# Recurrent attention and a gated feed-forward in one kernel: state matmuls ordered behind scores, one step begun by halves, the last rows stored in two parts, and a planner that counts changes of tile shape

## The chip, the cores and the metric

The kernel runs on one core of one Trainium2 chip. The metric is device time in microseconds (us), here the median of three runs. The core has five engines with instruction queues of their own that work side by side: TensorE (PE in the profile), VectorE (DVE), ScalarE (ACT), GpSimd (POOL) and SyncE (SP). PE multiplies matrices and writes to eight banks of PSUM; DVE, ACT and POOL work element by element; SP (and, for the weights, POOL) issues the DMA transfers. Each queue runs in its order; an instruction that waits for a semaphore holds up all that is behind it on its queue.

## The reference

First a linear recurrence per batch, head and feature, over 768 tokens, then a gated feed-forward over all tokens. There are 4 batches, 8 heads of width 48, and d_ff is 1536. Cut to what is computed:

```python
f = 1.0 / (1.0 + np.exp(-f_logit))
for t in range(S):
    state = f[:, :, t, :, None] * state + np.einsum('bhd,bhe->bhde', k[:, :, t], v[:, :, t])
    y[:, :, t] = np.einsum('bhd,bhde->bhe', q[:, :, t], state)
x = y.transpose(0, 2, 1, 3).reshape(B * S, H * D)          # 3072 x 384
out = (np.maximum(x @ w_gate, 0.0) * (x @ w_val)) @ w_out  # 3072 x 384
```

## The kernel before

The recurrence is done in chunks of 128 tokens. Within a chunk, cumulative sums of the log decay (the "cum" matmuls, L612, L613, L784) go through exponentials on ACT (`expo`, L625, L628, L794, L796), which scale keys and queries to `hats` (POOL L630, L806, L809; DVE L633). Keys and queries are transposed to `qkT`, in the first pass by PE (L664), later by DMA on SP (`turn`, L563). Scores are keys against queries (`scores`, L703 and L851), masked by DVE into `ptm` (L708, L858). Outputs come from masked scores and values (L736, L890) and from queries and the old state (`inter`, L719, and L886). The state is renewed by keys against values (`state`, L685 and L913), an addition on DVE (`ssum`, L581) and a multiply on POOL (`st`, L583).

The work is staged in six steps, `c` from 0 to 5 (the loop at L988). Each step makes 512 rows of `x`, transposed in `xT`, and runs the feed-forward over them: `ffn_hidden` for 12 blocks of d_ff (two groups of three matmuls at L937, relu on ACT at L943, product on DVE at L947 into `gT`), then `ffn_out` (12 matmuls at L966 for each of four blocks of 128 rows, a copy on ACT at L976, a store on SP at L980 from one of four buffers `osb`). Steps 0 to 3 get their rows from `attention_unit(d, b)`, which covers two chunks, 256 tokens, of one batch: pass `d` = 0 is steps 0 and 1, pass `d` = 1 is steps 2 and 3, with two units to a step. Steps 4 and 5 use `attention` for one chunk of all four batches. In steps 0 and 1 the feed-forward begins by halves (`groups`, L985): the first six blocks are done for the first unit's 256 columns, then for the second's, and the other six for all 512. The output part of a step is spread between the hidden blocks of the next one (`pend`); that of step 5 comes last.

No order is written out by hand. Every operation is added to a `Plan` with its engine, what it reads and writes, an occupancy and a latency in us, and a priority. `listed` (L181) then picks, again and again, the operation that can start earliest (ties by priority), on a model of five queues, the PSUM banks (with limits for each kind of use, L396) and the DMA rings; `needs` turns the result into semaphore waits. `chain` (L537) keeps operations of one line ("scores", "state", "intra", "ffn", ...) in order among themselves: each follows the one added before it. So the occupancies given at L691, L706, L748, L752, L755 and L851 decide how PE's work is interleaved, and, through it, the order on all other queues, the loads and stores of SP among them. Where the model has an early gap on PE, `fillers` puts matmuls on zeros (L1030).

Most matmuls use the array as one tile of 128 rows and 128 columns. The scores of a unit use 64x64 tiles, its state 64x128, `inter` 128x32, the outputs 64x32, and the scores of steps 4 and 5 64x128. In the model of this kernel a change from one tile shape to another costs nothing by itself; each operation's occupancy holds its own share.

`new_state(kv[0], ...)` is called right after the state matmuls are added; the state's second half, `new_state(kv[1], ...)`, at the end of the unit.

Of the kernel before, what the change touches and what calls it, by code (L numbers as in the profile page):

```python
# [11 lines left out]
class Op:  # L12
# [4 lines left out]
                 "after", "follows", "flow", "goal", "floor", "ring", "descs", "deps0", "ways")  # L17

    def __init__(self, eng, emit, reads, writes, occ, lat, prio, opens=(), after=(), follows=()):
        self.eng, self.emit, self.reads, self.writes = eng, emit, reads, writes  # L20
        self.occ, self.lat, self.prio, self.opens = occ, lat, prio, list(opens)
        self.after, self.follows = list(after), list(follows)
        self.users = []
        self.inc = False
        self.sem = None
        self.val = 0
        self.start = None
        self.flow = None
        self.ring = "hw"
        self.descs = 0  # L30
        self.floor = 0.0
        self.ways = {eng: (emit, occ, 0.0)}

# [81 lines left out]
class Plan:  # L115
# [9 lines left out]
    def add(self, eng, emit, reads=(), writes=(), occ=0.5, lat=0.2, prio=0, opens=(), after=(), follows=()):  # L125
        op = Op(eng, emit, list(reads), list(writes), occ, lat, prio, opens, after, follows)
        op.idx = len(self.ops)
        self.ops.append(op)
        return op
# [51 lines left out]
    def listed(self, banks, rings):  # L181
# [20 lines left out]
        left = len(self.ops)  # L202

# [8 lines left out]
        while left:  # L212
# [19 lines left out]
            op.eng, op.emit, op.occ = e, op.ways[e][0], op.ways[e][1]  # L232
            for tile, s in zip(op.opens, slot):
                if s["tile"] is not None:
                    for o in s["tile"].ops:
                        op.deps[o] = "war"
                s["tile"] = tile
                tile.ap, tile.slot = s["ap"], s
                used[tile.group] = used.get(tile.group, 0) + 1
# [80 lines left out]
def bass_hgrn2_outer__then__ffn_reglu_kernel(  # L320
# [216 lines left out]
    def chain(line, *args, **kw):  # L537

        last = tails.get(line)
        tails[line] = add(*args, follows=[last] if last else [], **kw)  # L540
        return tails[line]
# [44 lines left out]
    def attention_unit(d, b):  # L586
# [93 lines left out]
        def state():  # L680
            for p in range(NP):
# [8 lines left out]
        chain("state", "PE", state, hk_(h0) + hk_(h0 + 1) + [f"hats{h0 + i}" for i in range(2)] + [f"v_{v0 + i}" for i in range(2)],  # L690
              kv, occ=0.54, lat=PE_L, prio=P + 4, opens=kv)  # L691
        dk = [f"decu_{b}{j}" for j in range(2)]
        new_state(kv[0], 2 * d, b, w0, P, decu[:, b, 0, :, :], dk)
        pk = []
        for i in range(2):
# [10 lines left out]
            chain("scores", "PE", scores, [k_ for k_ in both if k_[-2] == "0" or k_.startswith(f"qkT{q0 + i}_")], sj, occ=0.29 if i else 0.38, lat=PE_L, prio=P + 5, opens=sj)  # L706
            for j in range(2):
# [4 lines left out]
                pk.append(f"ptm{m0 + i}_{j}")  # L712
        ys = [Bank("y"), Bank("y")]
# [32 lines left out]
        if late:  # L746
            chain("intra", "PE", outputs, both + old + [f"S{b}_0"] + pk + [f"{x}{v0 + i}" for x in ("v_", "vpad") for i in range(2)], ys,
                  occ=1.17 if d else 1.06, lat=PE_L, prio=P + 7, opens=ys)  # L748
        for half in range(0 if late else 2):
            chain("intra", "PE", lambda half=half: intra(half), pk[2 * half:2 * half + 2]  # L750
                  + [f"v_{v0 + half}", f"vpad{v0 + half}"] + (ys if half else []), ys,
                  occ=0.44 if half == 0 else 0.35, lat=PE_L, prio=P + 7, opens=ys if half == 0 else [])  # L752
        if not late:
            chain("inter", "PE", lambda: inter(1), both + [f"S{b}_0", ys[1]], [ys[1]],
                  occ=0.28, lat=PE_L, prio=P + 7)  # L755
# [76 lines left out]
    def attention(c, b):  # L832
# [9 lines left out]
        if b % 2 == 0:  # L842
# [11 lines left out]
            chain("scores", "PE", scores, qk_(qi) + qk_((w + 1) % NQ), both, occ=0.66, lat=PE_L, prio=P + 5, opens=both)  # L854
# [103 lines left out]
    def ffn_out(g, bs, cuts=1):  # L958
        gi = g % NG
        o = {b: Bank("f") for b in bs}  # L960
        for s in range(NJ // OJ):
            js = range(s * OJ, (s + 1) * OJ)
            for b in bs:
                def proj_out(b=b, js=js):
                    for j in js:
                        mm = te.matmul(o[b].ap[:, 0:DM], gT[gi][:, j, b * C:(b + 1) * C], wo[:, j, :],  # L966
                                       start=(j == 0), stop=(j == NJ - 1))
                    return mm
                P = (g + 1) * B * 10 + 5 + NJ * 3 + b * 3
                chain("ffn", "PE", proj_out,  # L970
                      [f"gT{gi}_{j}_{b}" for j in js] + sorted({w_key("wo", j) for j in js}), [o[b]],
                      occ=pe_t(*[DM] * OJ), lat=PE_L, prio=P + 1000, opens=[o[b]] if s == 0 else [])
        for b in bs:
            oi = (g * B + b) % NO
            P = (g + 1) * B * 10 + 5 + NJ * 3 + b * 3
            add("ACT", lambda b=b, oi=oi: sc.activation(osb[oi][:, :], o[b].ap[:, 0:DM], AF.Copy), [o[b]], [f"osb{oi}"],  # L976
                prio=P, **act_t(DM))
            row = ((2 * (g % 2) + b // 2) * S + (g // 2 * 2 + b % 2) * C) if g in units else b * S + g * C
            both = [(bass.AP(tensor=out.tensor, offset=row * DM, ap=[[DM, C], [1, DM]]), osb[oi][:, :])]
            op = add("SP", lambda both=both: [sy.dma_start(d, s_) for d, s_ in both], [f"osb{oi}"], [f"out{g}_{b}"],  # L980
                     occ=0.5, lat=0.9, prio=P)
            dma(op, f"osb{oi}", 0.7, len(both), 130)
# [3 lines left out]
              1: [(0, 2, range(0, 6)), (2, 4, range(0, 6)), (0, 4, range(6, NJ))]}  # L986
# [30 lines left out]
    for item in pend:  # L1017
        ffn_out(*item)
# [98 lines left out]
```

## Time and profile before

| | us |
|---|---|
| runs | 194.48, 194.25, 194.47 (median 194.47) |
| the profiled execution | 194.1 |
| its span | 192.4 |
| TensorE busy, share of the span | 183.7, 95% |
| VectorE, ScalarE, GpSimd busy | 109.5, 109.9, 67.6 |
| granted TensorE clock over the span | 1.0 |

The profile shows one execution. The span runs from the first to the last instruction; the execution's time has about 1.7 us around it. Busy times of engines lie beside one another and do not add up to the span. The ends of matmuls are modelled and overlap, so that a block's cost is the distance from its start to the next one's. A line such as "L937 PE MATMUL ps<-xT,wg 128*128 128x512 bf16 x3" names the line of the kernel, the engine, the output and inputs by the program's names, the tile (rows * columns), the moving operand's shape and the number of instructions. Most busy groups of the page, with mean durations:

| group | count | busy us | mean ns |
|---|---|---|---|
| L937 PE, hidden, gate and value, 512 columns | 360 | 97.4 | 379 |
| L937 PE, hidden, 256 columns | 144 | 23.6 | 273 |
| L966 PE, output, 384 columns | 288 | 52.1 | 326 |
| L736 PE, outputs of the units, tile 64x32 | 512 | 6.1 | 220 |
| L703 PE, scores, tile 64x64 | 256 | 5.1 | 219 |
| L685 PE, state, tile 64x128 | 128 | 4.2 | 204 |
| L719 PE, `inter`, tile 128x32 | 144 | 3.5 | 221 |
| L976 ACT, output copy, 384 columns | 24 | 11.8 | 490 |

### The profile page before, as it was taken

How to read it: one execution, taken by the hardware profiler on the slowest of the kernel's cores; microseconds unless marked ns; L12 is line 12 of the kernel's file. 1: busy time of each engine (PE TensorE's matmuls, PEld its weight loads, DVE VectorE, ACT ScalarE, POOL GpSimd, SP SyncE). 2: the span in 40 equal slices, each digit the busy share in tenths (PEclk: the TensorE clock that was granted, in tenths of full speed). 3: DMA queues.
4: the chain of work that ended last, by engine and by line, in shares of the span. 5: the costliest groups of instructions: out<-in, count | busy, mean ns of one | idle time of the engine just before them, and what ended most of it. 6: DMA issues, size and time to landing. Idle time of an engine off the chain costs nothing.

```text
span 192.4 us, 5447 instructions
## 1 busy us (share of the span) xinstructions
PE 183.7 (95%) x2291; PEld 108.9 (57%) x2291; DVE 109.5 (57%) x203; ACT 109.9 (57%) x232; POOL 67.6 (35%) x108
## 2 busy tenths in 40 slices
PE   7779797999999999999999999999999999999994
PEld 7657493556688645555556545555555455554552
DVE  5377555765899998965556546337238233344200
ACT  3867783468698777367396395485434433334322
POOL 8759460316465545435538408108100000000000
PEclk9999999999999999999999999999999999999999
DMA  5999999999959999997999889998540311011122
GB/s 159 316 257 266 245 207 210 243 260 278 280 102 264 211 253 209 234 201 160 215 171 198 171 188 227 157 207 191 88 95 29 85 41 39 2 41 41 44 81 82
DMA packets 93864, 32.46 MB, mean 169 GB/s; under 512 B 86928, under 2 KB 93840, under 8 KB 93840
## 3 DMA queue, kind: packets, MB, share of 16 engines
q1 hardware_dynamic: 89856, 28.58, 66.3%
q0 software_dynamic: 3984, 3.54, 11.3%
q8 instruction: 18, 0.29, 0.6%
q14 instruction: 6, 0.05, 0.1%
HBM read 25.95 MB, written 4.72 MB: 159 GB/s over the span
## 4 chain that ended last, share of the span: by engine, by line
PE 82%; DMA 12%; SPq 2%; POOL 1%; issue 0%; ACT 0%
PE ps L937 45%; PE ps L966 25%; DMA wv<-in_moe_w_val_dram 5%; DMA k_in<-in_k_dram 4%; DMA wg<-in_moe_w_gate_dram 3%; SPq L486 2%; PE ps L736 2%; PE ps L703 2%; PE ps L685 1%; PE ps L719 1%; PE ps L851 1%; POOL hats L630 1%; PE ps L890 1%; PE ps L664 1%; PE ps L886 1%; PE ps L784 1%
## 5 line engine op out<-in xcount | busy, mean ns | idle before, releaser
L947 DVE TENSOR_TENSOR gT<-relu,ps 128x512 bf16<-128x512 bf16 (+1 forms) x84 | 50.3, 607 | 54.2 <-PE ps L937 46.1
L943 ACT ACTIVATE relu<-ps 128x512 bf16<-128x512 f32 (+1 forms) x84 | 44.7, 536 | 31.5 <-PE ps L937 30.6
L937 PE MATMUL ps<-xT,wg 128*128 128x512 bf16 (+1 forms) x252 | 60.5, 349 | 1.2 <-DMA wg<-in_moe_w_gate_dram 0.9
L937 PE MATMUL ps<-xT,wv 128*128 128x512 bf16 (+1 forms) x252 | 60.5, 349 | 1.0 <-DMA wv<-in_moe_w_val_dram 1.0
L966 PE MATMUL ps<-wo,gT 128*128 128x384 bf16 x288 | 52.1, 326 | 0.0
L966 PEld LDWEIGHTS ps<-wo,gT 128*128 128x128 bf16 x288 | 27.1, 98 | 19.0
L937 PEld LDWEIGHTS ps<-xT,wv 128*128 128x128 bf16 x252 | 23.4, 98 | 21.4 <-DMA wv<-in_moe_w_val_dram 1.5
L937 PEld LDWEIGHTS ps<-xT,wg 128*128 128x128 bf16 x252 | 23.6, 98 | 19.9 <-DMA wg<-in_moe_w_gate_dram 1.1
L976 ACT ACTIVATE osb<-ps 128x384 f32<-128x384 f32 x24 | 11.8, 490 | 31.5 <-PE ps L966 31.5
L708 DVE TENSOR_TENSOR ptm<-ps,seen 128x512 bf16<-128x512 f32 x32 | 20.0, 680 | 3.2 <-PE ps L703 3.2
L630 POOL TENSOR_TENSOR hats<-k_in,expo 128x384 bf16<-128x384 f32 x16 | 15.9, 998 | 10.5 <-ACT expo L625 8.2
L583 POOL TENSOR_TENSOR st<-ssum,decu 128x384 bf16<-128x384 f32 x12 | 9.9, 830 | 18.4 <-DVE ssum L581 12.2
L806 POOL TENSOR_TENSOR hats<-k_in,expo 128x384 bf16<-128x384 f32 x8 | 7.8, 996 | 21.1 <-DMA k_in<-in_k_dram 17.2
L858 DVE TENSOR_TENSOR ptm<-ps,tri 128x512 bf16<-128x512 f32 x16 | 10.1, 682 | 1.2 <-PE ps L851 1.2
L581 DVE TENSOR_TENSOR ssum<-ps,st 128x384 f32<-128x384 f32 x16 | 8.7, 552 | 2.6 <-PE ps L913 1.9
L760 ACT ACTIVATE xT<-ps 128x384 bf16<-128x384 f32 x11 | 6.5, 606 | 5.7 <-PE ps L736 5.6
L639 POOL CAST vpad<-v_in 128x384 bf16<-128x384 f32 x16 | 8.5, 557 | 0.1
L601 ACT ACTIVATE f_in<-f_in 128x768 f32<-128x768 f32 (+1 forms) x9 | 6.8, 768 | 2.8 <-DMA f_in<-in_f_logit_dram 2.7
L809 POOL TENSOR_TENSOR hats<-q_in,expo 128x384 bf16<-128x384 f32 x8 | 7.8, 994 | 0.0
L633 DVE TENSOR_TENSOR hats<-q_in,expo 128x384 bf16<-128x384 f32 x8 | 7.7, 960 | 0.1
L625 ACT ACTIVATE expo<-ps 128x384 f32<-128x384 f32 x12 | 5.5, 488 | 3.2 <-PE ps L613 3.2
L603 ACT ACTIVATE bneg<-f_in 128x768 bf16<-128x768 f32 (+1 forms) x9 | 6.8, 768 | 0.1
(86 smaller groups left out, 166.8 us busy)
## 6 DMA issues: line engine op xcount, KB each, us to landing
f_in<-in_f_logit_dram SPq DMA_DIRECT2D x12, 384.0 KB, 5.1
k_in<-in_k_dram SPq DMA_DIRECT2D x12, 384.0 KB, 5.5
q_in<-in_q_dram SPq DMA_DIRECT2D x12, 384.0 KB, 5.6
v_in<-in_v_dram SPq DMA_DIRECT2D x12, 384.0 KB, 5.0
out_dram<-osb SPq DMA_DIRECT2D x24, 192.0 KB, 2.0
wo<-in_moe_w_out_dram POOLq DMA_DIRECT2D x3, 384.0 KB, 8.8
wg<-in_moe_w_gate_dram POOLq DMA_DIRECT2D x2, 288.0 KB, 6.5
wv<-in_moe_w_val_dram POOLq DMA_DIRECT2D x2, 288.0 KB, 7.2
```

The costliest lines, as they stand in the source:

```text
L581: add("DVE", lambda: ve.tensor_tensor(tmp[:, :], kv.ap[:, 0:HD], s_old[:, :], ALU.add), [kv, f"S{b}_{(c + 1) % 2}"], [key], prio=P + 8, ** ...
L583: add("POOL", lambda: gp.tensor_tensor(t4(s_new), t4(tmp), rate, ALU.mult), [key] + dk, [f"S{b}_{c % 2}"], prio=P + 8, occ=0.79, lat=0.23)
L630: add("POOL", lambda i=i, hi=hi, ei=ei: gp.tensor_tensor(hats[:, hi, 1, :, 0:D], by_i["k"][:, i, :, :], expo[:, ei, 1, :].rearrange("p (h ...
L639: add("POOL", lambda i=i, vout=vout: gp.tensor_copy(vout, by_i["v"][:, i, :, :].rearrange("p (n j) d -> p n j d", j=2)), key["v"] + [f"vpa ...
L708: add("DVE", lambda i=i, j=j, s=sj[j]: ve.tensor_tensor(ptm_all[:, m0 + i, j, :, :], s.ap[:, :].rearrange("p (n t) -> p n t", n=NP), seen[ ...
L806: add("POOL", lambda: gp.tensor_tensor(hk, kin[:, b % 2, :, :], ex[:, 1, :].rearrange("p (h d) -> p h d", h=H), ALU.mult), in_keys("k", c, ...
L858: add("DVE", lambda j=j, s=s: ve.tensor_tensor(ptm[mi][:, j, :, :], s.ap[:, :].rearrange("p (n t) -> p n t", n=NP), mask, ALU.mult), [s, " ...
L937: mm = te.matmul(bank.ap[:, 0:n], wt[:, kt, j * 128:(j + 1) * 128], xT[xi][:, b0:b1, kt, :], start=(kt == 0), stop=(kt == NK - 1))
L943: add("ACT", lambda: sc.activation(relu[ri][:, 0:n], gate.ap[:, 0:n], AF.Relu), [gate], [f"relu{ri}"], prio=P, **act_t(n))
L947: add("DVE", lambda: ve.tensor_tensor(gT[gi][:, j, n0:n1], relu[ri][:, 0:n], val.ap[:, 0:n], ALU.mult), [val, f"relu{ri}"], [f"gT{gi}_{j}_ ...
L966: mm = te.matmul(o[b].ap[:, 0:DM], gT[gi][:, j, b * C:(b + 1) * C], wo[:, j, :], start=(j == 0), stop=(j == NJ - 1))
L976: add("ACT", lambda b=b, oi=oi: sc.activation(osb[oi][:, :], o[b].ap[:, 0:DM], AF.Copy), [o[b]], [f"osb{oi}"], prio=P, **act_t(DM))
```

## The change

Five things change, all of them on the host, in what is added to the plan and what the plan reckons.

- An operation carries a tile shape. When the plan places an operation on PE whose shape differs from the last one's, it adds 0.095 us to its occupancy if the last was 128x128 and 0.14 us otherwise. The occupancies of the narrow operations are lowered in return.
- In pass 1 (steps 2 and 3) the state matmuls of a unit are added after its scores and must follow the last scores in the order (`behind`).
- Step 2's feed-forward begins by halves: its first three blocks of d_ff are done for the first unit's 256 columns, then for the second's, and the other nine for all 512.
- The last block of output rows (step 5, fourth block) is computed, copied and stored in two column parts, 0 to 192 and 192 to 384, each with its own bank, copy and store.
- `ffn_out` loops over parts, and the keys of `osb` and of the stores name the part; for the other blocks there is one part, 0 to 384.

```diff
+    def add(self, eng, emit, reads=(), writes=(), occ=0.5, lat=0.2, prio=0, opens=(), after=(), follows=(), tile="128x128"):
         op = Op(eng, emit, list(reads), list(writes), occ, lat, prio, opens, after, follows)
+        op.tile = tile
...
             op.eng, op.emit, op.occ = e, op.ways[e][0], op.ways[e][1]
+            if e == "PE" and op.tile != shape:
+                op.occ += 0.095 if shape == "128x128" else 0.14
+                shape = op.tile
...
-    def chain(line, *args, **kw):
+    def chain(line, *args, behind=(), **kw):
         last = tails.get(line)
-        tails[line] = add(*args, follows=[last] if last else [], **kw)
+        tails[line] = add(*args, follows=([last] if last else []) + list(behind), **kw)
...
-        chain("state", "PE", state, hk_(h0) + hk_(h0 + 1) + [f"hats{h0 + i}" for i in range(2)] + [f"v_{v0 + i}" for i in range(2)],
-              kv, occ=0.54, lat=PE_L, prio=P + 4, opens=kv)
         dk = [f"decu_{b}{j}" for j in range(2)]
-        new_state(kv[0], 2 * d, b, w0, P, decu[:, b, 0, :, :], dk)
+
+        def states():
+            chain("state", "PE", state, hk_(h0) + hk_(h0 + 1) + [f"hats{h0 + i}" for i in range(2)] + [f"v_{v0 + i}" for i in range(2)],
+                  kv, occ=0.315, lat=PE_L, prio=P + 4, opens=kv, tile="64x128",
+                  behind=[tails["scores"]] if d else [])
+            new_state(kv[0], 2 * d, b, w0, P, decu[:, b, 0, :, :], dk)
+        if not d:
+            states()
...
-            chain("scores", "PE", scores, [...], sj, occ=0.29 if i else 0.38, lat=PE_L, prio=P + 5, opens=sj)
+            chain("scores", "PE", scores, [...], sj, occ=0.215, lat=PE_L, prio=P + 5, opens=sj, tile="64x64")
...
+        if d:
+            states()
...
-                  occ=1.17 if d else 1.06, lat=PE_L, prio=P + 7, opens=ys)
+                  occ=0.94 if d else 0.8, lat=PE_L, prio=P + 7, opens=ys, tile="64x32")
...
-                  occ=0.44 if half == 0 else 0.35, lat=PE_L, prio=P + 7, opens=ys if half == 0 else [])
+                  occ=0.26, lat=PE_L, prio=P + 7, opens=ys if half == 0 else [], tile="64x32")
...
-                  occ=0.28, lat=PE_L, prio=P + 7)
+                  occ=0.14, lat=PE_L, prio=P + 7, tile="128x32")
...
-            chain("scores", "PE", scores, qk_(qi) + qk_((w + 1) % NQ), both, occ=0.66, lat=PE_L, prio=P + 5, opens=both)
+            chain("scores", "PE", scores, qk_(qi) + qk_((w + 1) % NQ), both, occ=0.43, lat=PE_L, prio=P + 5, opens=both, tile="64x128")
...
-    def ffn_out(g, bs, cuts=1):
+    def ffn_out(g, bs, cuts=(0, DM)):
         gi = g % NG
-        o = {b: Bank("f") for b in bs}
-        for s in range(NJ // OJ):
+        parts = list(zip(cuts, cuts[1:]))
+        o = {(b, z): Bank("f") for b in bs for z in parts}
+        steps = [(s, b, z) for z in parts for s in range(NJ // OJ) for b in bs]
+        for s, b, z in steps:
...
-                        mm = te.matmul(o[b].ap[:, 0:DM], gT[gi][:, j, b * C:(b + 1) * C], wo[:, j, :],
-                                       start=(j == 0), stop=(j == NJ - 1))
+                    mm = te.matmul(o[b, z].ap[:, 0:z[1] - z[0]], gT[gi][:, j, b * C:(b + 1) * C], wo[:, j, z[0]:z[1]],
+                                   start=(j == 0), stop=(j == NJ - 1))
...
-              1: [(0, 2, range(0, 6)), (2, 4, range(0, 6)), (0, 4, range(6, NJ))]}
+              1: [(0, 2, range(0, 6)), (2, 4, range(0, 6)), (0, 4, range(6, NJ))],
+              2: [(0, 2, range(0, 3)), (2, 4, range(0, 3)), (0, 4, range(3, NJ))]}
...
-        ffn_out(*item)
+        ffn_out(*item, cuts=(0, DM) if item != pend[-1] else (0, 192, DM))
```

## The prediction

> **What bounds the kernel now.** I read the page's totals first, then the chain of waits in order of time, then TensorE's timeline, then the tail.
>
> ```profile
> PE 183.7 (95%) x2291; PEld 108.9 (57%) x2291; DVE 109.5 (57%) x203; ACT 109.9 (57%) x232; POOL 67.6 (35%) x108
> PE 82%; DMA 12%; SPq 2%; POOL 1%; issue 0%; ACT 0%
> ```
> TensorE (PE) is busy 95% of 192.4 us; no other engine passes 57%. The chain (start, length, what) says where that holds:
>
> ```profile
> 21.32 9.57 DMA wv<-in_moe_w_val_dram
> 30.89 0.05 issue
> 30.94 3.41 PE ps L937 x15
> ...
> 181.71 7.81 PE ps L966 x48
> 189.53 0.02 issue
> 189.55 0.49 ACT osb L976
> ```
> Between 30.94 and 189.53 every piece of the chain is PE's. So there are three stretches: a head that ends when the last third of `wv` lands (30.89), 158.6 us in which only PE's own work counts, and a tail of 2.8 us.
>
> TensorE's timeline (start, duration, work) gives the price of a change of tile shape:
>
> ```profile
> 29.14 0.81 PE L937 MATMUL ps<-xT,wg 128*128 128x512 bf16 x3
> 30.94 0.82 PE L937 MATMUL ps<-xT,wv 128*128 128x512 bf16 x3 [0.98 <-DMA wv<-in_moe_w_val_dram]
> 46.67 1.46 PE L966 MATMUL ps<-wo,gT 128*128 128x384 bf16 x8
> 48.06 0.52 PE L685 MATMUL ps<-vpad,hats 64*128 64x96 bf16 x16
> 48.51 0.64 PE L703 MATMUL ps<-qkT 48*64 48x128 bf16 x32
> 49.08 0.82 PE L966 MATMUL ps<-wo,gT 128*128 128x384 bf16 x4
> 49.74 0.33 PE L612 MATMUL ps<-bneg,upto 128*128 128x384 bf16 x1
> 79.77 0.81 PE L937 MATMUL ps<-xT,wg 128*128 128x512 bf16 x3
> 80.51 0.51 PE L685 MATMUL ps<-vpad,hats 64*128 64x96 bf16 x16
> 80.96 0.82 PE L937 MATMUL ps<-xT,wv 128*128 128x512 bf16 x3
> ```
> Starts are to be read, since ends overlap. Three full matmuls of 512 columns advance the start by 0.65, but 79.77 to 80.51 is 0.74: entering a narrow tile costs 0.09. The first block after leaving is 0.01 longer (49.08 to 49.74 is 0.66, four 384-column matmuls elsewhere 0.65). From 48.06 to 48.51 one narrow block follows another of a different shape in the same 0.45 that L685 takes before a full-width block (80.51 to 80.96). So a narrow block next to a narrow block saves 0.104.
>
> **The change, part by part.**
>
> *Narrow blocks together.* With the new plan's instruction order beside the old one, I count after 30.94 how often PE goes from full width to narrow: 20 times before, 17 after (in three of the four units of pass 1 the state matmuls stand directly behind the scores, in the fourth behind the outputs, where before one of four stood beside scores). 3 x 0.104 = -0.31 us. Bounds: 3 x 0.09 and, if the new neighbours cost as much as a separate entry, 0.
>
> [...]
>
> *Step 2 by halves.* Three of the twelve blocks of d_ff are done per unit, 256 columns at a time: six groups (gate and value) become twelve of half width. Three 256-column matmuls take 0.328 (27.51 to 27.84 on the same timeline), three of 512 take 0.648: 6 x (2 x 0.328 - 0.648) = +0.05 on PE. The finer start gains nothing by itself, since PE has no idle time there to fill. Beside PE: ACT +6 x 0.386 - 3 x 0.596 = +0.53 and DVE +6 x 0.416 - 3 x 0.684 = +0.44. DVE is 80 to 90% busy from 48 to 82 us, but the new order brings 24 output matmuls (L966, no DVE work) into 75.7 to 80.3, so the load spreads; taken as hidden.
>
> *Last rows in two parts.* 12 matmuls of 384 columns (0.1625 each, 7.81/48) become 24 of 192. The 192-column matmuls at L612 start 0.08 apart: 24 x 0.0825 - 1.95 = +0.03. Then only the second half is exposed. ACT: 490 ns for 384 columns, 176 for 8 (L652), so 192 cost about 333: -0.16. The store:
>
> ```profile
> 190.40:190.80 0.40, 0.00 (x0) 0.00 (x0) 0.00 (x0) 0.00 (x0) 0.00 (x0) 1.00 0.00 0
> 190.80:191.00 0.20, 0.00 (x0) 0.00 (x0) 0.00 (x0) 0.00 (x0) 0.00 (x0) 1.00 0.39 154
> 191.00:191.20 0.20, 0.00 (x0) 0.00 (x0) 0.00 (x0) 0.00 (x0) 0.00 (x0) 1.00 1.03 392
> 191.20:191.40 0.20, 0.00 (x0) 0.00 (x0) 0.00 (x0) 0.00 (x0) 0.00 (x0) 1.00 1.03 384
> 191.40:191.60 0.20, 0.00 (x0) 0.00 (x0) 0.00 (x0) 0.00 (x0) 0.00 (x0) 1.00 0.17 54
> 191.60:192.00 0.40, 0.00 (x0) 0.00 (x0) 0.00 (x0) 0.00 (x0) 0.00 (x0) 1.00 0.00 0
> ```
> (Window, length, engines, clock, DMA share, GB/s.) Of the 2.3 us from ACT's end (190.04) to 192.4 the DMA engines work only about 0.6; the rest is fixed. Half the bytes per row in equally many rows: between 0 saved (if a row costs the same) and 0.3. I take -0.25. The first half's store is issued about 1 us earlier; an issue takes 0.34 on SP, so the second is not delayed.
>
> [...] Here four stores at L980 stand at 73.31, 73.98, 76.36 and 76.83 on SP and landed a median of 2.0 after issue, the last two plainly overlapped; so I take one fixed cost.
>
> *Planner's costs.* These move instructions but no work. Head: in the new order both halves of a unit's outputs (L736) stand behind the group that waits for `wg` at 21.07, so 0.33 of PE work moves behind that wait; POOL places its state multiply (0.84) after the first `wo` issue, which delays the key product at 24.32 by 0.84 and the transposes at 25.65 by perhaps 0.5. The cover is the 0.98 that PE idles for `wv` at 30.94. That transfer is issued at 21.32 on POOL's landing of `wg`, ahead of all that moved. Without the cover it would be +0.3 to +0.5; I take 0.
>
> *Waits that the new order can open after 30.94.* The four transposes that stood at 45.13 now come 0.65 earlier, at 44.48, and need the key product that POOL ends at 44.40: 0 to 0.2. State behind scores makes the state late: scores, four masks on DVE, `ssum` (L581), POOL's L583, then L719. From the start of scores: 0.29 + 0.22 (first half and its latency) + 2.47 (four L708) + 0.55 + 0.83 = 4.36. PE's work between, summed from the rows in the new order, is 4.9 in unit 0 and 4.7 in unit 1; unit 2 has 5.4 against 4.7 (one more gT product), unit 3 stands about 0.25 clear. Nothing stalls, but margins are 0.25 to 0.7. Old small stall for comparison: L719 at 72.90 starts 0.05 later than its entry price explains. I take +0.10 in all, bounds 0 and 0.9 (all four late by half a us, less their margins, and the four transposes).
>
> **Sum.** -0.31 + 0.05 + 0.03 + 0.10 - 0.16 - 0.25 = -0.54. The profiled execution took 194.1 (span 192.4, 1.7 around it), so 193.56; it lies 0.37 under the median 194.47, so in runs of that kind 193.93. Bounds of this case: 193.6 (no new wait, 0.3 at the store) to 194.5.
>
> **Rivals.**
>
> *The state's margin is eaten.* If DVE's masks and POOL's product come 0.5 later than summed (L630 on POOL takes 998 ns against L583's 830, DVE is near full), units 1 and 3 stall 0.15 and 0.25 and the transposes 0.1: +0.4 over my 0.1, 194.3. Against: the old order had equally tight places and lost 0.05.
>
> *Slower: step 4's first scores (L851) wait for their transposed keys and queries.* SP's order changes: the loads of q and v for step 4, and the next f, now stand behind the fourth output block of step 1, which ends on PE at 86.6; ACT 0.49, store 0.36, q issued at 87.5, landed 5.6 later at 93.1. The step's cumulative sums move from 86.1 to 91.5, so POOL's products begin at about 92.4, and the last input to a transpose is ready at 97.6. Its DMA transpose stands behind a k load (about 98) and lands 3.0 / 3.6 / 6.4 us after issue (least, median, most in the trace); an issue itself took up to 3.6. Scores stand at 104.6 on my sum, against 100.5. With median values there are 3 us left; with an issue at 100.5 and the longest landing it is 106.9, 2.3 late: 196.2. It turns slower from a landing at about 105.5. For it: loads fill the queue; against: scores themselves moved 4.1 later.
>
> *The change does not do what it says:* real neighbours cost as much as apart (the 0 bound), and only the tail gains: 194.25.
>
> **How the numbers follow.** My case 0.55, margin eaten 0.20, scores wait 0.15, tail alone 0.10. What a measurement can tell is 0.2%, 0.39 us: faster is below 194.08, slower above 194.86. My case is almost all faster, with a little of the fourth: 0.57; same 0.27 (the second, most of the fourth, the rim of mine); slower 0.16 (the third and the end of the second). Predicted 193.93; its own range 193.6 to 194.5; the range for 8 in 10 reaches into the slower rival to 195.2 and, for a landing of `wv` or a store that is luckier, down to 193.4.
>
> **What would show it.** Right: the chain still all PE from about 30.9, PE's last matmul at 189.3 to 189.4, narrow entries 17, the last ACT piece 0.33, the end about 2.4 after it begins. Wrong: a wait named at L719 (state) or L851 (transposes) on PE, idle over 0.98 before `wv`, or a last store that ends no sooner.

## The result and the profile after

| | before | after |
|---|---|---|
| runs, median us | 194.48 (7 runs) | 193.82 (7 runs, 193.47 to 193.93) |
| ratio after / before | | 0.9964, 95% interval 0.9952 to 0.9976 |
| profiled execution, its span | 194.1, 192.4 | 193.93, 192.2 |
| head: first group of 512 columns on `wv` starts | 30.94 | 31.45 |
| TensorE from there to the last output copy | 158.61 | 158.31 |
| tail: from that copy's start to the end of the span | 2.82 | 2.43 |

The changed kernel is 0.36% faster. The three lines at the bottom split each profiled span at the two places that the prediction used. They add up to -0.18, not to the -0.66 of the medians: before's profiled execution was one of its faster ones, after's one of its slower ones.

Totals and chain shares on the page of after (all lines are of `kernel.py` after the change: the hidden matmuls L937 are L950 now, the output L966 is L981, scores L703 L714, state L685 L691, `inter` L719 L732, warming L1030 L1046):

```profile
PE 185.4 (96%) x2326; PEld 114.5 (60%) x2326; DVE 109.1 (57%) x205; ACT 110.7 (58%) x237; POOL 68.3 (36%) x108
PE 91%; DVE 3%; ACT 2%; DMA 2%; issue 1%
```

The 12% of DMA in the chain are down to 2%: the head no longer ends with the landing of `wv`. TensorE's timeline of after shows what it ends with (start, duration, work, and in brackets the idle time ahead and what ended it):

```profile
26.19 0.39 PE L670 MATMUL ps<-ident,hats 128*128 128x128 bf16 x4
26.41 0.27 PE L950 MATMUL ps<-xT,wg 128*128 128x256 bf16 x1
27.63 0.39 PE L950 MATMUL ps<-xT,wg 128*128 128x256 bf16 x2 [0.94 <-issue]
...
30.80 0.81 PE L950 MATMUL ps<-xT,wg 128*128 128x512 bf16 x3
31.45 0.81 PE L950 MATMUL ps<-xT,wv 128*128 128x512 bf16 x3
```

TensorE stops for 0.94 us between the first and the second matmul of one group. They read the same tiles, and the second has no semaphore to wait for; the profile names nothing ("issue"). The `wv` group follows at 31.45 with no wait in front of it. Before, it waited 0.98 and started at 30.94.

After the head, the same timeline in step 2, with a narrow pair:

```profile
81.53 1.46 PE L981 MATMUL ps<-wo,gT 128*128 128x384 bf16 x8
82.93 0.64 PE L714 MATMUL ps<-qkT 48*64 48x128 bf16 x32
83.50 0.51 PE L691 MATMUL ps<-vpad,hats 64*128 64x96 bf16 x16
83.95 0.82 PE L981 MATMUL ps<-wo,gT 128*128 128x384 bf16 x4
```

Eight output matmuls take 1.30 by themselves and 1.40 here: one entry. Scores then take 0.57, as they did ahead of a full-width block (before, 78.53 to 79.11 was 0.58), and the state 0.45, as before: the second entry is gone and nothing has come in its place.

The end of the chain (start, length, what), and the windows of the tail (window, length, engines, clock, DMA share, GB/s):

```profile
181.90 7.84 PE ps L981 x60
189.74 0.02 issue
189.76 0.33 ACT osb L991
```
```profile
190.10:190.50 0.40, 0.00 (x0) 0.00 (x0) 0.00 (x0) 0.00 (x0) 0.00 (x0) 1.00 0.48 158
190.50:190.90 0.40, 0.00 (x0) 0.00 (x0) 0.00 (x0) 0.00 (x0) 0.00 (x0) 1.00 0.00 0
190.90:191.10 0.20, 0.00 (x0) 0.00 (x0) 0.00 (x0) 0.00 (x0) 0.00 (x0) 1.00 0.56 196
191.10:191.30 0.20, 0.00 (x0) 0.00 (x0) 0.00 (x0) 0.00 (x0) 0.00 (x0) 1.00 0.87 288
191.30:192.20 0.90, 0.00 (x0) 0.00 (x0) 0.00 (x0) 0.00 (x0) 0.00 (x0) 1.00 0.01 2
```

The copy takes 0.33. The DMA engines work twice, once for each part; the second burst lies within 0.4 us where the whole rows took 0.6. From the copy's end to the end of the span there are 2.1 us, 2.3 before.

So two of three stretches gained about as worked out, and the head lost half a us that the prediction had put at 0. The experiments ask what the stop at 27.63 is, and whether each part is worth what the ledger says.

### The profile page after: what moved, and what is told of

The parts are those of the page before. It is cut to its first block, busy times and chain, and to the rows that moved or that the text cites. A ratio compares the mean times of both kernels' runs of the same rounds, so it can differ in the third digit from the quotient of the medians.

```text
span 192.2 us, 5529 instructions
## 1 busy us (share of the span) xinstructions
PE 185.4 (96%) x2326; PEld 114.5 (60%) x2326; DVE 109.1 (57%) x205; ACT 110.7 (58%) x237; POOL 68.3 (36%) x108
## 4 chain that ended last, share of the span: by engine, by line
PE 91%; DVE 3%; ACT 2%; DMA 2%; issue 1%
PE ps L950 49%; PE ps L981 25%; PE ps L749 3%; DVE ptm L719 3%; PE ps L670 2%; PE ps L714 2%; DMA f_in<-in_f_logit_dram 2%; PE ps L618 1%; PE ps L691 1%; PE ps L1046 1%; PE ps L732 1%; PE ps L619 1%; PE ps L864 1%; ACT xT L773 1%; PE ps L903 1%
## 5 line engine op out<-in xcount | busy, mean ns | idle before, releaser
L960 DVE TENSOR_TENSOR gT<-relu,ps 128x512 bf16<-128x512 bf16 (+1 forms) x87 | 50.9, 592 | 53.3 <-PE ps L950 41.5
L950 PE MATMUL ps<-xT,wg 128*128 128x512 bf16 (+1 forms) x261 | 61.2, 343 | 1.3 <-issue 0.9
L950 PE MATMUL ps<-xT,wv 128*128 128x512 bf16 (+1 forms) x261 | 61.0, 342 | 0.0
L981 PE MATMUL ps<-wo,gT 128*128 128x384 bf16 (+1 forms) x300 | 51.5, 320 | 0.0
L981 PEld LDWEIGHTS ps<-wo,gT 128*128 128x128 bf16 x300 | 28.2, 98 | 17.9
L950 PEld LDWEIGHTS ps<-xT,wv 128*128 128x128 bf16 x261 | 24.8, 98 | 20.0
L950 PEld LDWEIGHTS ps<-xT,wg 128*128 128x128 bf16 x261 | 24.2, 98 | 19.6 <-issue 1.2
L991 ACT ACTIVATE osb<-ps 128x384 f32<-128x384 f32 (+1 forms) x25 | 12.0, 478 | 34.6 <-PE ps L981 34.6
L719 DVE TENSOR_TENSOR ptm<-ps,seen 128x512 bf16<-128x512 f32 x32 | 19.9, 682 | 3.1 <-PE ps L714 3.1
L645 POOL CAST vpad<-v_in 128x384 bf16<-128x384 f32 x16 | 9.1, 591 | 0.1
L1046 PE MATMUL ps<-zeros 128*128 128x64 bf16 (+1 forms) x107 | 8.1, 253 | 0.0
L1046 PEld LDWEIGHTS ps<-zeros 128*128 128x128 bf16 x107 | 7.2, 129 | 0.2
```

The source lines that it names most:

```text
L645: add("POOL", lambda i=i, vout=vout: gp.tensor_copy(vout, by_i["v"][:, i, :, :].rearrange("p (n j) d -> p n j d", j=2)), key["v"] + [f"vpa ...
L719: add("DVE", lambda i=i, j=j, s=sj[j]: ve.tensor_tensor(ptm_all[:, m0 + i, j, :, :], s.ap[:, :].rearrange("p (n t) -> p n t", n=NP), seen[ ...
L950: mm = te.matmul(bank.ap[:, 0:n], wt[:, kt, j * 128:(j + 1) * 128], xT[xi][:, b0:b1, kt, :], start=(kt == 0), stop=(kt == NK - 1))
L960: add("DVE", lambda: ve.tensor_tensor(gT[gi][:, j, n0:n1], relu[ri][:, 0:n], val.ap[:, 0:n], ALU.mult), [val, f"relu{ri}"], [f"gT{gi}_{j}_ ...
L981: mm = te.matmul(o[b, z].ap[:, 0:z[1] - z[0]], gT[gi][:, j, b * C:(b + 1) * C], wo[:, j, z[0]:z[1]], start=(j == 0), stop=(j == NJ - 1))
L991: add("ACT", lambda b=b, z=z, oi=oi: sc.activation(osb[oi][:, z[0]:z[1]], o[b, z].ap[:, 0:z[1] - z[0]], AF.Copy), [o[b, z]], [f"osb{oi}_{z ...
```

## The experiments

Every kernel was run in 11 or 12 executions (a_more_warm in 6), beside before on the same chip, but not all on one chip (medians of before there: 194.17 to 194.43). The ratio with its interval is taken over the runs of both kernels and is not the quotient of the two medians. Each kernel has one profile, and the ledger gives head, TensorE's stretch and tail of that one execution as above. All compute the whole output.

| kernel | median us | ratio to before, 95% interval | head | TensorE | tail |
|---|---|---|---|---|---|
| after_again | 193.96 | 0.9982 (0.9965 to 0.9999) | 31.49 | 158.31 | 2.44 |
| b_tail | 193.88 | 0.9974 (0.9955 to 0.9993) | 31.08 | 158.89 | 2.43 |
| a_whole_tail | 194.43 | 1.0006 (0.9989 to 1.0023) | 31.49 | 158.40 | 2.83 |
| a_old_costs | 194.59 | 1.0025 (0.9999 to 1.0051) | 31.11 | 158.93 | 2.44 |
| a_fewer_warm | 193.96 | 0.9983 (0.9965 to 1.0002) | 31.47 | 158.39 | 2.43 |
| a_more_warm | 196.43 | 1.0100 (1.0068 to 1.0133) | 34.60 | 158.32 | 2.43 |
| a_no_halves | 194.72 | 1.0018 (0.9998 to 1.0037) | 31.25 | 159.26 | 2.45 |
| a_state_first | 194.22 | 0.9997 (0.9980 to 1.0014) | 31.28 | 158.74 | 2.43 |
| a_shift | 193.43 | 0.9941 (0.9915 to 0.9967) | 30.55 | 158.37 | 2.42 |
| a_shift_288 | 193.64 | 0.9977 (0.9952 to 1.0003) | 31.00 | 158.32 | 2.41 |
| o_shift | 193.80 | 0.9979 (0.9957 to 1.0002) | 32.77 | 158.45 | 2.43 |
| b_shift | 194.89 | 1.0004 (0.9974 to 1.0035) | 30.83 | 159.45 | 2.83 |

### after_again: the changed kernel a second time

> The changed kernel once more, unchanged, for a second trace of it. Ledger of the first traces against before: head +0.51 (first 512-column group on wv at 31.45 instead of 30.94), PE from there to its last matmul -0.28, tail -0.40; sum -0.17, but the medians of the runs differ by -0.66. Theory A: the head's +0.51 is an accident of that one execution (half-speed matmuls until about 10.7 us, a stall of 0.94 at 26.4 to 27.6 inside one group) and not the change's; then the median is 0.65 (0.5 to 0.8) below before, and in this trace the first 512-column wv group starts at 30.8 to 31.0, with PE idle for the landing of wv ahead of it; PE from there 158.3, tail 2.44. Rival B: the new order makes the head late by 0.5 every time, and before's first trace was a lucky one; then the group starts at 31.4 to 31.5 again without a wait for wv, with the stall at the same place, and the other two stretches as in the first trace.

The head is 31.49 again, with the stop in the same place of the same group:

```profile
26.49 0.27 PE L950 MATMUL ps<-xT,wg 128*128 128x256 bf16 x1
27.67 0.39 PE L950 MATMUL ps<-xT,wg 128*128 128x256 bf16 x2 [0.91 <-issue]
```

Half of theory A falls: the head's loss is not an accident. Its other half is answered too: in this execution the matmuls ran at full speed from the start (the 22 warming matmuls at 6.70 are 0.056 apart; in the first trace 0.107), and the head ended at the same time. B is right about the head, wrong about before: the head is 30.94, 31.08 and 31.11 in the traces of before, b_tail and a_old_costs, all with the old head order. The ratio, 0.9982, is nearer to 1 than the first, 0.9964; the intervals overlap.

### b_tail and a_whole_tail: the last rows alone, and all but them

b_tail is before with the new `ffn_out` and, in the last line, `cuts=(0, DM) if item != pend[-1] else (0, 192, DM)`. a_whole_tail is after with

```diff
-        ffn_out(*item, cuts=(0, DM) if item != pend[-1] else (0, 192, DM))
+        ffn_out(*item, cuts=(0, DM))
```

> Before, with the last block of rows alone computed, copied and stored in two column parts; the order of everything else is before's (20 entries into narrow tiles, 103 warming matmuls). Theory: the tail falls from 2.84 to 2.44, PE gains 24 matmuls of 192 for 12 of 384 (+0.03): -0.37 in the runs (bounds -0.25 to -0.45). Rival: a store's fixed part is paid for each of the two in a row or the smaller store ends no sooner: tail 2.7 to 2.85 (only ACT's 0.16 gained), runs 0 to -0.13. Should the whole of the 0.66 come from the tail, this kernel would be 0.66 below before.

> The changed kernel with its last block of rows in one part as before; its order is otherwise unchanged (17 entries, step 2 by halves). Theory: head 0, PE -0.28 without the 0.03 of the split, so -0.3 against before in the runs (-0.15 to -0.4), with a tail of 2.84. Rival 1 (the split does nothing by itself): as fast as the changed kernel, -0.66. Rival 2 (the order of the rest is worth nothing, or the head is late by 0.5): 0 to +0.2.

The tail goes with the split alone: 2.82 and 2.83 without it, 2.43 and 2.44 with it. That is -0.39 in every pair, and the runs differ by -0.47 between after_again and a_whole_tail. The rival of a second fixed cost falls. b_tail's runs gained 0.29 by the medians (ratio 0.9974), inside its bounds, though its TensorE stretch was 0.28 longer than before's in the profiled execution: 0.18 of that is one wait that ends at 80.89, where the state matmuls need a `vpad` that GpSimd made late (L639) because its load of `v` landed late in that execution (L639 idle 1.9 for loads of `v` on its page), and 0.03 is the split. a_whole_tail is not faster than before: with the head at 31.49, the gain of TensorE's stretch is given away, as its rival 2 said.

### a_old_costs: the planner's costs taken back

```diff
-            if e == "PE" and op.tile != shape:
-                op.occ += 0.095 if shape == "128x128" else 0.14
-                shape = op.tile
```
and all `occ` of the narrow operations as before.

> The changed kernel with the planner's old occupancies and no cost for a change of tile: state behind scores, step 2 by halves and the two-part tail stay. The instruction order has 17 entries into narrow tiles as the changed kernel, and the head of before (103 warming matmuls, outputs on both sides of the group that waits for wg). Theory A (planner's costs are worth 0 in the head): the same time as the changed kernel, -0.66 against before (-0.5 to -0.8). Rival B (the planner's costs make the head late by 0.5): 0.3 to 0.5 faster than the changed kernel, about -1.1 against before, with the first 512-column wv group at 30.9 here and at 31.45 there. Rival C: the gain on PE comes from the planner's costs and not from state behind scores; then PE's stretch is 158.6 here and not 158.3, and the runs show -0.35.

The head is before's again, 31.11, so the planner's costs do move it by 0.4. But the kernel is not faster than the changed one; it is 0.6 slower by the medians (0.24 between the two profiled executions: head -0.38, TensorE's stretch +0.62). Its trace has another stop, in step 2, between two hidden groups:

```profile
79.15 0.50 PE L949 MATMUL ps<-xT,wg 128*128 128x256 bf16 x3
79.98 0.49 PE L949 MATMUL ps<-xT,wv 128*128 128x256 bf16 x3 [0.32 <-DVE ptm L718]
```

0.83 from start to start where 0.33 is the rule. The name in brackets is only the last semaphore: the group's weight load had started at 79.39, and the first matmul behind it, which waits for none, came 0.59 later. None of the three expectations had this, and the run did not separate them; o_shift, further down, is the same order without the stop.

### What the stops have in common

I numbered TensorE's recorded instructions (weight loads, matmuls, semaphore instructions) in the order of their starts, and set beside them the 16 KB transfers that the trace lists as "instruction" on a queue of their own (q8 on the page of after: 18 transfers, 0.29 MB); that page has 2326 matmuls and as many weight loads, 258 of the two for each transfer. Stops without a semaphore stand at these numbers (number modulo 256 in brackets):

```
kernel         stop ends  at instruction   transfer starts  stop ends after
after_again    19.34      705  (193)       16.96            2.38
after_again    27.67      961  (193)       25.33            2.34
a_old_costs    79.98     2753  (193)       77.64            2.34
a_fewer_warm   15.25      449  (193)       12.84            2.41
a_more_warm    19.57      705  (193)       17.16            2.41
a_more_warm    27.59      961  (193)       25.34            2.25
b_shift        66.26     2241  (193)       63.66            2.60
b_shift        74.15     2497  (193)       71.83            2.32
```

Every stop stands at a multiple of 256 behind the others, and ends 2.3 to 2.6 us after one of these transfers begins. I call an instruction with such a number (193 modulo 256) a boundary. The later rows are from the next two groups of runs, which were made to test this. The other traces with the new head and its boundaries where they were (after, a_whole_tail, a_no_halves, a_state_first) stop at instruction 961 too, at 27.4 to 27.7 and 2.2 to 2.4 us after a transfer's start.

Most boundaries pass without a stop. The traces of before and after have 18 each: in before TensorE stops at none, in after at two, 0.24 us at instruction 705 (it ends at 20.27, 2.38 after a transfer's start) and the 0.94 at 961. The count of 256 and the times behind a transfer's start are what the traces show; what an instruction at a boundary waits for they do not name.

### a_fewer_warm and a_more_warm: the boundary moved, the work left alone

TensorE's first warming matmuls on zeros (`fillers`) made wider and fewer, or narrower and more, for the same warming time:

```diff
-        gap, (n, each) = op.start - at, (64, 0.06) if at < 6.0 else (128, 0.054)
+        gap, (n, each) = op.start - at, (103, 0.0965) if at < 6.0 else (128, 0.054)
```
and (51, 0.0478) for a_more_warm.

> The changed kernel with 39 warming matmuls of 103 columns in place of the first 63 of 64 columns: the same warming time, the same order, but every later instruction of TensorE stands 24 matmuls (48 instructions, with the weight loads) earlier in its queue. In the three traces of the new head TensorE stops without a semaphore in its way at 27.63 to 27.67, inside a group of three matmuls, and each time at the same count of its instructions; 253 or 256 instructions before there is a smaller stop, and 16 KB instruction transfers start between, one for each 256 instructions. Theory A (the queue runs out of fetched instructions at a boundary of 256): the boundary moves 24 matmuls later in the program; by the traces it is asked for at about 29.2 and fetched by 27.7 to 29.2, so the stop is 0 to 0.2, TensorE waits for wv again, the first 512-column wv group starts at 30.9 to 31.1 instead of 31.45, and the time is 0.3 to 0.5 below the changed kernel. Theory B (the stop belongs to the data or to this place in the program: hats, wg, a PSUM bank): the stop stays at the second matmul of that group, 31.45 and the time stay.

> The changed kernel with 79 warming matmuls of 51 columns in place of the first 63 of 64: the same warming time, every later instruction of TensorE 16 matmuls (32 instructions) later in its queue. Theory A (boundary of 256 instructions, fetched too late): the boundary is met 16 matmuls earlier in the program, at about 24.9, while its transfer is started by the boundary before, which is met only about 0.7 earlier; so the stop is longer, 1.2 to 2.1, ending at 26.5 to 27.2 in the middle of 256-column groups before the transposes; the first 512-column wv group starts at 31.5 to 32.6 and the time is 0 to 1.1 above the changed kernel. Theory B (data or place): stop and time as in the changed kernel.

The stop went where the count went. In a_fewer_warm nothing stops at 27.6 any more; the stop stands one boundary earlier, which now falls into the fast matmuls of the first unit's outputs (TensorE's timeline, then its clock by windows):

```profile
13.77 0.40 PE L749 MATMUL ps<-ptm,vpad 64*32 64x128 bf16 x26 [0.18 <-DVE ptm L719]
15.25 0.30 PE L749 MATMUL ps<-ptm,vpad 64*32 64x128 bf16 x6 [1.08 <-issue]
```
```profile
15.00:18.50 3.50, 3.25 (x39) 0.51 1.22 285
18.50:22.00 3.50, 3.50 (x76) 1.00 1.27 238
```

So theory B falls, and theory A was right that the stop goes with the count and wrong about the gain: the boundary ahead of it had been left out of the expectation. On top, the granted clock fell to 0.51 for 3.5 us in this execution, and its head came out at 31.47 as before the move. In a_more_warm the stop grew from 0.91 to 2.31, the granted clock fell to 0.51 again, and the kernel lost 2.5 us by the medians:

```profile
25.02 0.27 PE L950 MATMUL ps<-xT,wg 128*128 128x256 bf16 x1
27.59 0.38 PE L950 MATMUL ps<-xT,wg 128*128 128x256 bf16 x2 [2.31 <-issue]
...
29.44 0.85 PE L950 MATMUL ps<-xT,wg 128*128 128x256 bf16 x3
```
```profile
28.50:32.00 3.50, 3.50 (x22) 0.51 1.22 208
```

Three matmuls of 256 columns take 0.64 there instead of 0.33. Not every execution has the slow clock: a granted clock of 0.99 over the span, as in these two profiles, stands in 3 of the 12 runs of a_fewer_warm and in 3 of the 6 of a_more_warm. The three runs of a_more_warm with it took 197.03 to 197.13, the three without it 195.03 to 195.82. So without the slow clock a_more_warm is 1.1 to 1.9 us above after_again's median, the most that I had (1.1) or more, and the slow clock, which the expectation had left out, adds the rest. What the head of a_fewer_warm is without it, no trace shows. The second stop of a_more_warm ended at the same time as in the changed kernel (27.59, against 27.63 and 27.67), as did the start of the transfer (25.34, against 25.40 and 25.33), though TensorE's last matmul ahead of it had started at 25.02, not at 26.41 and 26.49: in these three traces the end goes with the transfer and not with where TensorE stands.

### a_no_halves and a_state_first: the two parts on TensorE

a_no_halves leaves out group 2 of `groups`; a_state_first calls `states()` ahead of the scores for both passes, without `behind`.

> The changed kernel without step 2's beginning by halves: the planner then makes 16 entries into narrow tiles after the head instead of 17, and six groups of 512 columns stay whole. Theory: TensorE from the first 512-column wv group to the last output copy 158.31 - 0.104 - 0.05 = 158.15; head 31.45 and tail 2.44 as in the changed kernel; runs 0.15 below the changed kernel, unless an instruction boundary falls on a fast stretch. Rival 1 (halves fill a gap that opens without them): PE idle at the start of step 2, about 79 to 84, 0.2 to 1.0 longer. Rival 2 (entries cost nothing, the 0.28 has another cause): 158.26.

> The changed kernel with the state matmuls of pass 1 added ahead of the scores again, as before (tile costs in the plan, halves and two-part tail stay): 19 entries into narrow tiles after the head instead of 17. Theory (0.104 for each entry): TensorE's stretch 158.31 + 0.21 = 158.52, head and tail as in the changed kernel, runs 0.2 above it. Rival (entries cost nothing by themselves): 158.31 and the same time. Rival (state behind scores is what gains, through fewer waits): 158.6 and more.

a_state_first: two more entries, 158.74, which is the number of its second rival. One `inter` block starts 0.28 late by the spacing of starts (73.40) where 0.09 is an entry:

```profile
72.45 0.82 PE L947 MATMUL ps<-xT,wv 128*128 128x512 bf16 x3
73.40 0.52 PE L729 MATMUL ps<-qkT,st 128*32 128x128 bf16 x24
```

So 0.19 is a wait, for VectorE's last mask, which ends at 73.34. Without it the stretch is 158.55, 0.24 above 158.31: 0.12 for each entry against 0.104. The order with state behind scores gains in both ways, then, by fewer entries and by a wait that it avoids; the runs (0.9997 against 0.9982, intervals overlapping) do not tell the two kernels apart. a_no_halves: its theory (158.15) falls, and its rival 1 happened. Where the changed kernel has groups of 256 columns, TensorE waits for ScalarE:

```profile
75.29 0.34 PE L652 MATMUL ps<-halves,bneg 128*128 128x2 bf16 x8
76.42 0.82 PE L950 MATMUL ps<-xT,wg 128*128 128x512 bf16 x3 [0.78 <-ACT expo L634]
```

In the new order the finer start is worth 0.9 us of TensorE's stretch (158.31 with it, 159.26 without), and the ratio to before is 1.0018 without it, 0.9982 with it. In the changed kernel the same place has a group of 256 columns at 76.00 and no wait.

### a_shift, o_shift, b_shift: the boundary off the path

The warming matmuls widened in two places, so that early boundaries move by 8 matmuls and later ones by 17:

```diff
-        gap, (n, each) = op.start - at, (64, 0.06) if at < 6.0 else (128, 0.054)
+        gap, (n, each) = op.start - at, (73, 0.0684) if at < 6.0 else (128, 0.054) if at < 14.0 else (470, 0.19)
```

a_shift is the changed kernel with it, b_shift before with it. o_shift is a_old_costs with its first half, (73, 0.0684), alone. a_shift_288 is a_shift with the last rows cut at 288.

> The changed kernel with its warming matmuls on zeros made wider and fewer (55 of 73 columns for 63 of 64 in front, 3 of 470 for the later 11 of 128, the single one left out): the order of all other work is the changed kernel's. Boundaries of 256 instructions stand 8 matmuls later in the program up to the first unit's outputs and 17 later after them. By the changed kernel's own traces the third boundary is then met at about 21.7, behind the wait for wg, its successor is asked for at about 28 to 28.5 and, with 3.6 to 4.2 from the boundary to the start of the transfer and 2.35 from there to use, fetched by 27.6 to 28.3. Theory A (an instruction boundary met too early costs the head 0.5): no stop over 0.3 without a semaphore in TensorE's head, TensorE waits for wv again, first 512-column wv group at 30.9 to 31.1, its stretch 158.3, tail 2.44: 0.4 to 0.5 below the changed kernel, ratio to before 0.995 to 0.997. Rival B (the order of the head itself is late by 0.5, however its instructions are fetched): 31.45 and the changed kernel's time.

> The kernel a_shift with the last rows cut at column 288 instead of 192, so that only 96 columns stand behind the last matmul. Theory (what is exposed is the last part): the last copy on ScalarE 0.25 instead of 0.33 (from 490 ns at 384 and 333 at 192 columns), the store's bytes 0 to 0.12 shorter, TensorE's 24 matmuls of 288 and 96 columns within 0.02 of before: tail 2.25 to 2.36 instead of 2.44. Rival (rows of 384 bytes cost as much as rows of 768, or the first part's store, now later by 0.5 and larger, delays the second): tail 2.4 to 2.9.

> The kernel a_old_costs (state behind scores, halves and the two-part tail, planner's old costs) with 55 warming matmuls of 73 columns for 63 of 64, so that every boundary of 256 instructions stands 8 matmuls later in the program. There TensorE stopped for 0.48 at 79.98 between the weight load and the first matmul of a wv group, at an instruction whose count stands 7 x 256 behind that of the stop at 27.6 in the changed kernel. Theory (boundary): that stop is gone, TensorE's stretch is 158.4 to 158.5 instead of 158.93, head 31.0 to 31.2, tail 2.44: 0.4 to 0.5 below a_old_costs. Rival (a wait for a mask on VectorE, which the profile names there): the stop stays, and the time.

> Before, with the warming matmuls widened in the same way as in a_shift (55 of 73 columns in front, 2 of 470 for the later 7 of 128) and nothing else changed. In before's trace TensorE meets its third instruction boundary 0.0 to 0.2 and its fourth 0.5 after the transfer is usable, so no stop is there to be removed, and the head ends with the landing of wv. Theory A (a_shift gained by moving a boundary off the head's path): within 0.1 of before, first 512-column wv group at 30.6 to 31.1. Rival (fewer, wider warming matmuls make any head faster, through earlier loads): 0.4 to 0.5 below before, as a_shift against the changed kernel.

a_shift has no stop in the head, and TensorE waits for `wv` again:

```profile
29.54 0.81 PE L950 MATMUL ps<-xT,wg 128*128 128x512 bf16 x3
30.55 0.82 PE L950 MATMUL ps<-xT,wv 128*128 128x512 bf16 x3 [0.21 <-DMA wv<-in_moe_w_val_dram]
```

The head is 30.55, the stretch 158.37, the tail 2.42; the time is 193.43, ratio 0.9941 (0.9915 to 0.9967), the lowest of all. Theory A holds by the trace. By the runs its gain over the changed kernel is not sharp: the interval touches that of after_again, which ran on another chip, and a_shift_288, with the same head, has 0.9977 (0.9952 to 1.0003). The head came 0.35 earlier than the expectation's early end, since `wv` landed earlier in this execution; in a_shift_288, with the same head order, it was 31.00. In o_shift the stop at 79.98 is gone and the stretch is 158.45, as expected of the boundary and not of a mask:

```profile
80.82 0.50 PE L949 MATMUL ps<-xT,wg 128*128 128x256 bf16 x3
81.16 0.49 PE L949 MATMUL ps<-xT,wv 128*128 128x256 bf16 x3
```

Its runs go from a_old_costs's ratio of 1.0025 to 0.9979. For rival C of a_old_costs the stretch lies between the two numbers: of the 0.30 that TensorE gains in the changed kernel 0.16 stay without the planner's costs, and of the other 0.14, 0.09 is a wait of one `inter` block at 75.78 for GpSimd's state multiply, which the changed kernel does not have. o_shift's own head in the profiled execution, 32.77, is a late landing of `wv` and says nothing of the edit. b_shift is the control: its head stays with the landing of `wv`, 30.83, so wider warming matmuls alone speed nothing up. I had expected it within 0.1 of before; the stretch is 0.84 longer. Some 0.7 of that are two other boundaries that now fall into the outputs of units, at 66.26 and, shown here, at 74.15; another 0.1, in the outputs at 94.3, stands at no boundary, and its cause is not shown:

```profile
73.50 0.35 PE L736 MATMUL ps<-ptm,vpad 64*32 64x128 bf16 x20
74.15 0.57 PE L736 MATMUL ps<-ptm,vpad 64*32 64x128 bf16 x44 [0.30 <-issue]
```

Cutting at 288 shortened the last copy (0.25) but not the tail (2.41 against 2.42): the first part's store is issued at 189.25 and takes SP 0.33, and the last one follows at 189.63 with 0.43 where 0.33 is usual. The tail is where the rival had it; 192 is no worse a cut.

## Why the prediction was right, and where it was not

*Narrow blocks together, -0.31; halves +0.05; split +0.03; new waits +0.10.* Their sum for TensorE's stretch was -0.13; it measured -0.30, the same 158.31 in both traces of the changed kernel. Without the 0.10 for waits the sum is -0.23. The waits did not come: neither the transposes nor any `inter` block waits in the changed kernel, and the 0.05 that before lost at L719 is gone. The price of an entry held (pairs in the timeline; a_state_first 0.12).

*Step 2 by halves: "The finer start gains nothing by itself, since PE has no idle time there to fill."* This step failed, without harm to the sum. It read before's idle time, but the part stands in another order: there the 512-column start waits 0.78 for ScalarE (a_no_halves).

*Last rows in two parts, -0.41 in the tail.* Measured -0.39, in every pair of the table with and without the split. One fixed cost, as taken. A fixed cost paid twice would have made a longer tail; no run shows one.

*Planner's costs, 0, covered by the 0.98 that TensorE idles for `wv`.* This is the step that failed in size: +0.51 and +0.55 in the two traces. The cover was counted against late data alone. The stop at the boundary 961, which the first trace meets at 26.4 and leaves at 27.6, 2.2 after a transfer's start, used it up and more. TensorE's part of the chain therefore ends at 189.74, not at the 189.3 to 189.4 that the prediction had named as its sign. That "without the cover it would be +0.3 to +0.5" came near that size for another reason. a_old_costs (31.11, old costs) and a_shift and a_shift_288 (30.55 and 31.00, new costs, boundary moved), which all wait for `wv` again, show that the new order of the head costs nothing by itself.

*From the profiled execution to the runs.* I carried over that before's profiled execution lies 0.37 under its median. After's lay 0.11 above its own. In the ledger of the profiled executions I was off by +0.51 in the head and by -0.17 on TensorE; by that ledger the change is worth -0.18, where the prediction had -0.54. That 193.93 met 193.82 is in part luck: before's profiled execution was one of its faster ones, and after_again's runs, against another set of before's, gained 0.21 by the medians, not 0.66.

*Rivals.* The margin of the state was not eaten. The scores of step 4 start at 105.21 on time, with no wait at L864. "Tail alone" is not it: a_whole_tail shares the stretch of 158.4. What I had no rival for is the one that a_more_warm shows, a slower kernel with the same work in the same order: its three runs without the slow clock took 195.03 to 195.82 (before on that chip 194.27), and its trace has the stop of 2.31.

*Open.* When a transfer starts is not settled. Nor is why a boundary stops TensorE: what the expectations say of it was my theory, and the traces show the counts and the times alone. From meeting the boundary at 18.9 to 19.8 to the next transfer it is 4.5 to 5.1 us in the old head and 5.6 to 6.3 in the new one. In the new head TensorE waits for `wg` some 20 instructions behind that boundary, in the old one some 75 behind it, so the later start may go with that wait; this is a guess. But a_more_warm, with some 50, is as late as the new head, and b_shift, with as many, as early as the old one, and the other DMA traffic differs as well. No run tells these apart.

## What to carry to other kernels

Idle time ahead of a late load covers late data only once: before putting a moved edit at 0, list what else stands in that stretch, and TensorE's instruction boundaries (here 256 recorded instructions apart, weight loads included) are part of the list: the eight stops of the table, of 0.2 to 2.3 us, stood among matmuls of 96 to 256 columns, between 15 and 80 us. A stop marked "issue" inside a group of like matmuls was the sign of it in five of them (0.91 at 27.67 in after_again; in a_old_costs the profile put a semaphore's name there instead). Wider warming matmuls moved the boundary off the head (a_shift and a_shift_288, 30.55 and 31.00 against 31.49), but all the others with it (b_shift, two new stops, some 0.7), so each has to be looked at. And a part judged useless by before's idle times has to be judged in the order that the change makes.

## What the runs showed of the hardware

- The eight stops of the table, of 0.2 to 2.3 us, stood at TensorE instructions a multiple of 256 apart and ended 2.3 to 2.6 us after the start of a 16 KB instruction transfer. The changed kernel's work in the same order, with other warming matmuls alone, had a ratio to before from 0.9941 (a_shift) to 1.0100 (a_more_warm, half of its runs with a spell of slow clock).
- Beside a stop of TensorE of 1.08 and one of 2.31 us stand 3.41 us at half the granted clock (15.07 to 18.48 in a_fewer_warm and 28.55 to 31.96 in a_more_warm, in the trace's clock records). The first began 0.18 before its stop's end, the second 0.96 after it; TensorE was busy 1.88 and 1.10 of the 3.41 us ahead of them. That the stop is what leads to the spell is not shown: half of the runs of the one kernel and most of the other's lack it, and 14 of before's 110 runs beside the experiments have a granted clock of 0.99 or less too.
- The first trace of after and that of o_shift ran at half speed until about 10 us (warming matmuls of 128 columns 0.107 apart, not 0.056) though after_again, with the same warming as the first, ran at full speed; in the first it cost nothing that shows in the head (31.45, after_again 31.49), since the stop at 27.6 came later.
